# Output stores on ScalarE's queue, v loads on GpSimd's queue, SyncE's queue left to SBUF transposes, 16 matmul groups ahead

## The chip, the cores and the metric

One core of one Trainium2 chip. The metric is the time of one execution on the device in microseconds; a statement about a kernel is the median of several executions, or a ratio of executions taken in the same rounds on the same chip. An execution more than 1.5% above the fastest of the same kernel counts as slow here.

Some words used below: a hole is a stretch in which TensorE stands idle; a transfer lands when its completion semaphore is raised, and its landing time runs from issue to landing; half clock is a stretch in which the profile shows TensorE's granted clock at 0.5 (in before the median from start to start of the MLP's first-layer matmuls is 427 ns there and 216 ns at full clock); `vp` is GpSimd's multiplication of a pair's v by its weights; `osb` are the buffers of finished output tiles that the stores read.

## The reference

Attention with random features (8 batches x 8 heads, 576 tokens, head size 64, 128 features), whose output goes straight into a two-layer MLP over all 4608 tokens.

```python
def phi(x):
    proj = np.einsum('bhsd,md->bhsm', x, omega)
    h = proj - np.sum(x * x, axis=-1, keepdims=True) / 2.0
    h = h - np.max(h, axis=-1, keepdims=True)
    return np.exp(h) / np.sqrt(m)
q_p, k_p = phi(q_s), phi(k_s)
kv  = np.einsum('bhsm,bhsd->bhmd', k_p, v)
z   = np.sum(k_p, axis=2)
num = np.einsum('bhsm,bhmd->bhsd', q_p, kv)
den = np.einsum('bhsm,bhm->bhs', q_p, z)[..., None] + 1e-06
x   = (num / den)                       # -> (4608, 512)
h   = x @ w_in                          # 512 -> 2048
out = (h / (1 + np.exp(-1.702 * h))) @ w_out
```

## The kernel before

The 64 heads are worked as 32 pairs. Each pair needs its q and k transposed before the projection `K`/`Q` on TensorE. Pairs 0 to 7 are transposed by TensorE itself; from pair 8 (`TDMA`) on, SyncE transposes q,k from SBUF to SBUF by DMA (`TD`), and the attention output x as well (`XD`). k, q and the weights are loaded, and cast to bf16, by GpSimd's DMA queue; v (fp32) comes mostly on SyncE's queue, which also carries the output stores.

```python
XDMA, TDMA = 8, 8
...
LOADS += [(x, i) for i in range(8, NPAIR) for x in "kq"]     # GpSimd's order of loads
...
    for n, x in enumerate(LOADS):
        deps["ld", *x] = [("ld", *LOADS[n - 1])] if n else []
        if x[0] in "kq" and x[1] >= 8:                       # 8 buffers for q,k
            deps["ld", *x] += [("TD" if x[1] - 8 >= TDMA else "TQ", x[1] - 8)]
...
        def load_k(i):
            qk_t[i] = stq.tile([128, 2 * S], BF16, name="qk", tag="qk")
            nc.gpsimd.dma_start(qk_t[i][:, S : 2 * S], kv[i])
...
        def TD(i):
            t = qkp.tile([128, NS, 128], BF16, name="qkT", tag="qkT")
            st[i]["qkT"] = t
            nc.sync.dma_start_transpose(t[:], qk_t[i][:])
...
            elif kind == "vp":
                vp(a[0], eng)
                if a[0] + 8 < NPAIR:
                    load_v(a[0] + 8)                         # on SyncE
```

A static scheduler, run while the program is built, models each engine and fixes the order of all instructions. It interleaves the attention of coming pairs with the matmul groups of the MLP (9 blocks of 512 tokens), to keep TensorE full. `TD` of a pair may be placed only so many MLP groups ahead of the pair's due point (6 before, 16 after).

The softmax here doesn't subtract the row's maximum and nothing guards it: scores larger than these inputs give would overflow.

## Time and profile before

| | kernel before |
|---|---|
| time | 337.92 us, median of 3 (337.44 to 338.74) |
| profiled execution | span 340.0 us, TensorE busy 312.9 us, mean clock 0.984 |
| idle of TensorE up to its last matmul | 21.9 us, of which 5.27 before pair 8 |
| half clock of TensorE | 6.8 us from 62.6 us on |

The median transpose lands in 3.4 us. The tile's own view between 43 and 62 us (the first two transposes) gives another size, and the timeline of GpSimd (start us, us, what, and in brackets the idle time before it and who ended it) shows the loads that stood beside them:

```profile
L405 SPq DMA_TRANSPOSE qkT<-qk x2: 2341/3421/4501, 55.4 to 57.9; - x2
DMA to landing us min/median/max: 7.5/8.2/9.0
```
```profile
54.73 0.53 POOL L380 DMA_DIRECT2D qk<-in_k_dram  x1 [0.43 <-issue]
55.76 0.53 POOL L383 DMA_DIRECT2D qk<-in_q_dram  x1 [0.50 <-DMA qk<-in_q_dram]
64.93 0.53 POOL L380 DMA_DIRECT2D qk<-in_k_dram  x1 [8.64 <-DMA qkT<-qk]
```

Near the loads a transpose takes 7.5 to 9 us, not 3.4. And GpSimd issues no load from 56.3 to 64.9 us: the next k needs the buffer that this very transpose reads. While SyncE's transpose is under way, GpSimd's queue gets nothing new; the last load in it landed at 63.85 us.

### The profile page before, as it was taken

What the parts mean: (1) busy time and instruction counts of PE and PEld (TensorE: products, weight loads), DVE (VectorE), ACT (ScalarE), POOL (GpSimd) and SP (SyncE); (2) the same over time, 40 slices, a digit from 0 to 9 for tenths busy, and PEclk for the clock granted to TensorE, in tenths of its full rate; (3) what the DMA queues carried; (4) which work ended last, traced back from release to release, by engine and by line L of the source; (5) the groups of instructions that cost most, each with busy time, mean ns of one, the idle gap of its engine ahead of it and who ended that gap; (6) DMA issues with size and microseconds to landing.
All of it is one profiled execution on the core that took longest, in us unless ns stands there. A gap on an engine that the chain in (4) does not pass through costs nothing.

```text
span 340.0 us, 6567 instructions
## 1 busy us (share of the span) xinstructions
PE 312.9 (92%) x2516; PEld 152.9 (45%) x2562; DVE 181.6 (53%) x336; ACT 192.2 (57%) x353; POOL 79.7 (23%) x137
## 2 busy tenths in 40 slices
PE   5778999499978999999999999999999999999993
PEld 2444554144433445444444444444444444444441
DVE  2786985168854664555555555555564333334400
ACT  3766884286854676666666666666664444444411
POOL 7636423325431242222222111111110000000000
PEclk9899999699999999999999999999999999999999
DMA  7999999999999799686799444444422121112122
GB/s 199 286 222 269 198 221 247 179 149 218 157 186 157 139 175 197 133 160 142 143 135 179 93 87 85 89 85 87 85 53 50 39 55 31 33 31 61 31 64 62
DMA packets 68078, 44.27 MB, mean 130 GB/s; under 512 B 47504, under 2 KB 59536, under 8 KB 68048
## 3 DMA queue, kind: packets, MB, share of 16 engines
q1 hardware_dynamic: 54336, 28.46, 41.0%
q0 software_dynamic: 13712, 15.41, 27.4%
q8 instruction: 20, 0.33, 0.4%
q14 instruction: 10, 0.08, 0.1%
HBM read 36.73 MB, written 9.44 MB: 136 GB/s over the span
## 4 chain that ended last, share of the span: by engine, by line
PE 81%; DMA 9%; DVE 4%; ACT 2%; issue 2%; POOL 1%; ACTq 0%; DVEq 0%; POOLq 0%
PE mo L577 36%; PE mo L597 34%; DMA qkT<-qk 5%; PE pqk L448 3%; PE nd L539 3%; DMA qk<-in_q_dram 2%; PE pqk L477 2%; PE nd L521 2%; DMA xt<-xb 2%; DVE hm L492 1%; DVE xb L556 1%; PE tr L566 1%; ACT xt L428 1%; DVE m L496 0%; PE nd L453 0%
## 5 line engine op out<-in xcount | busy, mean ns | idle before, releaser
L591 DVE SCALAR_TENSOR_TENSOR gT<-th,mo 128x512 bf16<-128x512 bf16 x144 | 97.4, 679 | 99.5 <-ACT th L587 99.3
L577 PE MATMUL mo<-xt,win 128*128 128x512 bf16 x556 | 146.4, 383 | 3.7 <-DMA xt<-xb 1.4
L597 PE MATMUL mo<-wout,gT 128*128 128x512 bf16 x553 | 141.7, 381 | 2.2 <-DVE gT L591 0.9
L587 ACT ACTIVATE th<-mo 128x512 bf16<-128x512 f32 x144 | 86.1, 600 | 75.0 <-PE mo L577 73.0
L597 PEld LDWEIGHTS <-gT 128*128 128x128 bf16 x576 | 55.2, 98 | 67.4 <-issue 2.3
L577 PEld LDWEIGHTS <-win 128*128 128x128 bf16 x576 | 52.6, 98 | 63.7 <-issue 7.2
L486 ACT ACTIVATE qe<-pqk 128x1024 bf16<-128x1024 f32 x28 | 28.7, 1024 | 9.4 <-PE pqk L477 9.4
L466 ACT ACTIVATE ke<-pqk 128x1024 bf16<-128x1024 f32 x32 | 33.1, 1034 | 0.0
L510 POOL TENSOR_TENSOR vp<-v,em 128x576 bf16<-128x576 f32 x27 | 31.1, 1152 | 0.0
L380 POOL DMA_DIRECT2D qk<-in_k_dram x31 | 17.5, 565 | 55.6 <-DMA qkT<-qk 47.9
L607 ACT ACTIVATE osb<-mo 128x512 f32<-128x512 f32 x36 | 21.5, 598 | 15.6 <-PE mo L597 12.4
L509 POOL CAST vp<-em 128x9 bf16<-128x9 f32 x27 | 6.4, 236 | 101.1 <-DVE em L501 94.1
L556 DVE TENSOR_TENSOR xb<-nd,r 128x640 bf16<-128x640 f32 x30 | 24.7, 823 | 0.9
L496 DVE TENSOR_REDUCE m<-hm 128x9 f32<-128x576 bf16 x32 | 24.0, 749 | 0.3
L492 DVE TENSOR_TENSOR hm<-ke 128x576 bf16<-128x576 bf16 x32 | 17.8, 555 | 9.9 <-ACT ke L466 9.8
L457 ACT ACTIVATE ke<-nd 128x128 bf16<-128x128 f32 x32 | 8.9, 278 | 24.8 <-PE nd L454 24.1
L448 PE MATMUL pqk<-omT,qkT 64*128 64x128 bf16 x256 | 13.2, 224 | 7.6 <-DMA qkT<-qk 7.3
L383 POOL DMA_DIRECT2D qk<-in_q_dram x31 | 16.9, 545 | 9.5 <-DMA wout<-in_moe_w_out_dram 5.4
L539 PEld LDWEIGHTS <-qe 128*128 128x128 bf16 x320 | 13.8, 97 | 6.7 <-issue 0.7
L548 DVE RECIPROCAL r<-nd 128x10 f32<-128x10 f32 x30 | 6.4, 214 | 18.8 <-ACT qe L458 13.0
L521 PEld LDWEIGHTS <-ke 64*128 64x128 bf16 x576 | 12.5, 95 | 8.2 <-issue 2.5
L539 PE MATMUL nd<-kvs,qe 128*128 128x65 bf16 x300 | 14.3, 194 | 0.4
(54 smaller groups left out, 149.8 us busy)
## 6 DMA issues: line engine op xcount, KB each, us to landing
out_dram<-osb SPq DMA_DIRECT2D x72, 128.0 KB, 2.4
v<-in_v_dram SPq DMA_DIRECT2D x25, 288.0 KB, 5.5
qk<-in_k_dram POOLq DMA_DIRECT2D x31, 144.0 KB, 6.0
qk<-in_q_dram POOLq DMA_DIRECT2D x31, 144.0 KB, 6.3
win<-in_moe_w_in_dram POOLq DMA_DIRECT2D x4, 512.0 KB, 12.0
wout<-in_moe_w_out_dram POOLq DMA_DIRECT2D x4, 512.0 KB, 11.6
v<-in_v_dram POOLq DMA_DIRECT2D x7, 288.0 KB, 8.7
qkT<-qk SPq DMA_TRANSPOSE x24, 3.4
```

Source lines behind the costliest of these rows:

```text
L448: nc.tensor.matmul(pk[:, e, j * 128 : (j + 1) * 128], lhsT=t[64 * e : 64 * e + 64, k0 + j, :], rhs=omT[64 * e : 64 * e + 64, :],)
L466: nc.scalar.activation(out=st[i]["ke"][:, 1:9, :].rearrange("p (j e) f -> p e j f", e=2), in_=pk[:].rearrange("p e (j f) -> p e j f", f=12 ...
L486: nc.scalar.activation(out=dst, in_=src, func=AF.Exp, scale=SCALE)
L496: nc.vector.reduce_max(out=m[:], in_=st[i]["hm"][:], axis=AX.X)
L510: e.tensor_tensor(out=t[:, :, 0:64], in0=v_t[i][:], in1=em[:].unsqueeze(2).to_broadcast([128, NS, 64]), op=ALU.mult,)
L539: nc.tensor.matmul(nd[:, e, g * 65 : (g + 1) * 65], lhsT=qe[i % NQE][:, e, g * 128 : (g + 1) * 128], rhs=t[:, e, :],)
L556: nc.vector.tensor_tensor(out=xb[:].rearrange("p g e d -> p e g d"), in0=v4[:, :, :, 0:64], in1=r[:].unsqueeze(3).to_broadcast([128, 2, NG ...
L577: nc.tensor.matmul(dst, lhsT=win[:, c, f * 128 : (f + 1) * 128], rhs=xt[c][:, n * 512 : (n + 1) * 512], start=(c == 0), stop=(c == NC_ - 1),)
L587: nc.scalar.activation(out=t[:], in_=src, func=AF.Tanh, scale=0.851)
L591: nc.vector.scalar_tensor_tensor(out=gts[n][:, f, :], in0=t[:], scalar=1.0, in1=src, op0=ALU.add, op1=ALU.mult)
L597: nc.tensor.matmul(dst, lhsT=gts[n][:, f, r * 128 : (r + 1) * 128], rhs=wout[:, f, :], start=(f == 0), stop=(f == NFC - 1),)
L607: nc.scalar.activation(out=o[:], in_=src, func=AF.Copy, scale=0.5)
```

## The change

Intent: give SyncE's queue to the transposes alone, so that they go as soon as their data is there; start them earlier; and let loads and stores find their own queues. Core of the diff (hunk headers and some context left out):

```diff
+NOSB = 4
+NQK = 6
-LAT = {..., "S": 4.0}
+LAT = {..., "S": 3.0}
-    "TD": {"S": 0.6},
-    "XD": {"S": 0.6},
+    "TD": {"S": 2.1},
+    "XD": {"S": 1.2},
+    "st": {"A": 0.2},
-LOADS += [(x, i) for i in range(8, NPAIR) for x in "kq"]
+LOADS += [(x, i) for i in range(8, NPAIR) for x in "kqv"]
-            deps["TD", i] = ... + p("Q", i - 4) + p("K", i - 4) + l("k") + l("q")
+            deps["TD", i] = ... + p("Q", i - NQK) + p("K", i - NQK) + l("k") + l("q")
+                deps["st", n, r] = [("store", n, r)]
+        if x[0] == "v" and x[1] >= 8:
+            deps["ld", *x] += [("vp", x[1] - 8)]
-        if kind in ("TK", "TD") and begin[o[1]] - (6 if kind == "TD" else 0) > st["m"]:
+        if kind in ("TK", "TD") and begin[o[1]] - (16 if kind == "TD" else 0) > st["m"]:
-    qkp = ctx.enter_context(tc.tile_pool(name="qkp", bufs=4))
+    qkp = ctx.enter_context(tc.tile_pool(name="qkp", bufs=NQK))
-    osbp = ctx.enter_context(tc.tile_pool(name="osb", bufs=3))
+    osbp = ctx.enter_context(tc.tile_pool(name="osb", bufs=NOSB))
+        def send(n, r):
+            o = osb.pop((n, r))
             u = 2 * (4 * n + r)
             for h in range(2):
                 b, rank = divmod(u + h, NS)
-                nc.sync.dma_start(ov[b, SLOT[rank]], o[64 * h : 64 * h + 64, :])
+                nc.scalar.dma_start(ov[b, SLOT[rank]], o[64 * h : 64 * h + 64, :])
                 vp(a[0], eng)
-                if a[0] + 8 < NPAIR:
-                    load_v(a[0] + 8)
```

More of the change, by code (lines that the diff above doesn't have):

```diff
@@ L28 @@
 NQE = 4
+NOSB = 4
+NQK = 6
 NPAIR = B * 4
 SCALE = 1.0 / math.sqrt(math.sqrt(D))
-LAT = {"P": 0.26, "A": 0.20, "D": 0.16, "G": 0.20, "S": 4.0}
+LAT = {"P": 0.26, "A": 0.20, "D": 0.16, "G": 0.20, "S": 3.0}
 SELF = {"P": 0.0, "A": 0.11, "D": 0.13, "G": 0.10, "S": 0.0}
@@ L90, in schedule @@
         if i >= TDMA:
-            deps["TD", i] = (p("TD", i - 1) if i > TDMA else []) + p("Q", i - 4) + p("K", i - 4) + l("k") + l("q")
+            deps["TD", i] = (p("TD", i - 1) if i > TDMA else []) + p("Q", i - NQK) + p("K", i - NQK) + l("k") + l("q")
             t = p("TD")
@@ L149, in schedule @@
             if g == 3:
-                deps["store", n, r] = [o]
+                deps["store", n, r] = [o] + ([("st", *divmod(4 * n + r - NOSB, 4))] if 4 * n + r >= NOSB else [])
+                deps["st", n, r] = [("store", n, r)]
     for n, x in enumerate(LOADS):
         deps["ld", *x] = [("ld", *LOADS[n - 1])] if n else []
+        if x[0] == "v" and x[1] >= 8:
+            deps["ld", *x] += [("vp", x[1] - 8)]
         if x[0] in "kq" and x[1] >= 8:
@@ L603, in m2 @@
                 )
+        osb = {}
         def store(n, r, src):
             o = osbp.tile([128, DM], F32, name="osb", tag="osb")
+            osb[n, r] = o
             nc.scalar.activation(out=o[:], in_=src, func=AF.Copy, scale=0.5)
+        def send(n, r):
+            o = osb.pop((n, r))
             u = 2 * (4 * n + r)
@@ L680, in emit @@
                 {"KV": KV, "kvs": kvs, "ND": ND, "rd": rd, "xm": xm}[kind](a[0], t)
+            elif kind == "st":
+                send(*a)
             elif kind in ("TD", "XD"):
```

## The prediction

> **What bounds the kernel now.** I read the page first, its slices and then the chain. TensorE (PE) is busy 312.9 of 340.0 us, so only its idle or slow stretches are to be had; and the slices say where they lie.
>
> ```profile
> PE   5778999499978999999999999999999999999993
> PEclk9899999699999999999999999999999999999999
> DMA  7999999999999799686799444444422121112122
> ```
>
> A slice is 8.5 us. PE is below 9 in the first four, in the eighth (4 tenths, at a granted clock of 0.6), in the twelfth and in the thirteenth. From 110 us on it is full to the end. The DMA row is full over just the stretch where PE has holes. I then cut the span at the holes (columns: PE, PEld, DVE, ACT, POOL busy with counts, granted clock, DMA share and GB/s):
>
> ```profile
> 59.20:64.50 5.30, 0.06 (x2) 0.06 (x4) 0.00 (x0) 0.65 (x1) 0.00 (x0) 0.82 1.28 178
> 64.50:69.50 5.00, 5.00 (x21) 2.04 (x22) 1.36 (x3) 1.96 (x4) 2.65 (x5) 0.51 1.03 190
> 69.50:110.00 40.50, 35.49 (x373) 17.23 (x378) 27.48 (x50) 26.51 (x52) 14.05 (x23) 1.00 1.11 172
> 110.00:255.00 145.00, 143.40 (x1219) 71.12 (x1241) 84.43 (x157) 93.34 (x173) 32.42 (x52) 1.00 0.65 122
> ```
>
> One hole of 5.3 us, then 5.0 us of work at half clock, then 5.0 us of idleness spread over 40 us, then 1.6 us in 145. [...] Who ended the holes is in the waits of PE (total us, times, longest) and in the chain of waits (start, us, what):
>
> ```profile
> PE pqk L448 <- DMA qkT<-qk: 7.3, 2, 5.3
> PE mo L577 <- DMA xt<-xb: 1.4, 1, 1.4
> ```
> ```profile
> 55.42 8.98 DMA qkT<-qk
> 88.53 8.32 DMA qkT<-qk
> 100.29 5.66 DMA xt<-xb
> ```
>
> All three are SBUF transposes issued by SyncE: two of q,k (5.27 us before the work of pair 8, 2.04 us at 94.9), one of x (1.40 us at 104.6). The timeline of SyncE and GpSimd shows why the first came so late:
>
> ```profile
> 2.13 48.09 SPq L387 DMA_DIRECT2D v<-in_v_dram  x8
> 52.54 2.09 SPq L611 DMA_DIRECT2D out_dram<-osb  x2
> 54.74 0.51 SPq L387 DMA_DIRECT2D v<-in_v_dram  x1
> 55.42 9.26 SPq L405 DMA_TRANSPOSE qkT<-qk  x3
> ```
> ```profile
> 37.33 0.61 POOL L380 DMA_DIRECT2D qk<-in_k_dram  x1
> 37.93 0.55 POOL L383 DMA_DIRECT2D qk<-in_q_dram  x1
> ```
>
> The last two rows are k and q of pair 8; by the trace's landing events they arrived at 49.58 and 50.31. Their transpose could have gone then. It went at 55.42 (the first of the three merged in that row), because SyncE's queue is in order and first held a v load that waited for another pair's `vp`, two stores that waited for `osb`, and another v load. Then it took 8.98 us to land, against a median of 3.4 for this group, beside eight loads in flight.
>
> [...] So I expect nothing from bandwidth here, only from the order in SyncE's queue. The trace agrees so far as the lateness above was queue order. [...] the 5.27 us hole is followed by 0.51, the holes of 2.04 and 1.40 us by nothing. [...]
>
> **The change part by part.**
>
> *SyncE keeps only the 48 transposes.* It loses 72 store issues and 24 of its 25 v loads. The first transpose of pair 8 is then bound by its data. Six v loads (pairs 8 to 13, 295 KB each, 1.77 MB) no longer run before 50 us: loads of this size land 0.7 us apart at the quick stretches (pairs 6 and 7), so k and q of pair 8 arrive about 6 x 0.7 = 4 us earlier, near 46 us (estimate). With even 9 us to land, the transpose is there at 55, before PE asked for it at 59.2. So the 5.27 us hole goes (-5.3), and with it the half clock: 5.0 us of work at 0.51 becomes 2.5 (-2.5).
>
> *16 groups ahead, six buffers.* A matmul group of the MLP is 0.86 us, so 10 groups more are 8.6 us of earlier start, if k,q have landed and a buffer is free; six instead of four buffers permit it for pairs 8 to 13. I note that the static scheduler gates only the transpose by this number, not the projection K after it: K is placed as soon as the modelled transpose is over (2.1 + 3.0 us, before 0.6 + 4.0). So the attention of a pair moves ahead as a whole, and the room between transpose and use grows by only 0.5 us. What protects PE is that x of a block is ready some 8 us earlier: the 1.40 us wait for xt should go (-1.4). The 2.04 us wait should go because SyncE spent 86.7 to 94.6 on v, stores and transposes in turn, that transpose's own issue stretching to 2.90 us (-2.0).
>
> *v in the Pool queue, in the order k, q, v.* 24 issues of 0.55 us (row of GpSimd's v loads, 542 to 579 ns) are 13 us on an engine that is busy 79.7 of 340. It puts a v load, which waits for `vp` of eight pairs before, ahead of the next k; with about 8.4 us per pair and eight pairs in hand that wait is hidden. At the start it helps: today v of pairs 8, 9 and 10 is fetched at 2.6 to 13.2 us, ahead of q of pair 2, for which PE waits 1.15 us at 11.24. I count half of it (-0.6).
>
> *Stores on ScalarE.* Two issues of 0.47 to 0.59 us per tile, 1.12 us together, 36 times: 40 us more on ScalarE, busy 192.2, so 232 of 330, no bound by itself. What counts is how late it makes the next tanh. In the steady state a tanh follows the store's copy after 0.27 us idle; it would start about 0.9 us later. The PSUM bank that it frees is wanted again 1.66 us after its release there, and 0.86 us after it in the last 80 us. I worked these slacks out from the starts of L577 and the ends of L591 by bank. So the delay just fits[...]. The schedule reckons 0.2 us for what takes 1.1, so it won't plan around it: +1.0 in sum. *Four osb buffers* only let a store be sent later; 0.
>
> Late transposes that remain in the crowded 60 to 110 us: +1.5, from three landings of 7.5 to 10.5 us today among the first eight, of which only some hit PE.
>
> Sum: -5.3 -2.5 -2.0 -1.4 -0.6 +1.0 +1.5 = -9.3; 337.9 - 9.3 = 328.6 us.
>
> **Rivals.** *A: the waits come back elsewhere.* The DMA share is at 1.0 to 1.3 up to 110 us, and the change moves no byte out of the program: with attention 8 us earlier, transposes and loads crowd still more, and K is still placed 5.1 us behind its transpose. Against it: the six v loads leave the tightest stretch, and MLP work of block 1 is there to fill. It would leave 334 to 336. *B: ScalarE becomes the bound.* [...] tanh is 2.5 us late, over the 1.66 us of slack, and PE loses up to 0.8 us in each of some 17 periods between 110 and 255 us (8.42 us apart: store copies start at 197.69 and 206.11): up to +14, that is 338 to 342. For it: the phase is that close today. Against: the schedule shifts the phase, and one tight row seldom repeats so exactly. *C: no cost at all* (-11.8): 326.1, and 324 to 325 if the small waits for gT (0.64 and 0.25 us at 81 and 100 us) go too.
>
> **Range and chances.** The sure part is the hole and the clock, 7.8 us, by itself 2.3%: 330.1. The other gains (2.0, 1.4, 0.6) are 4.0, against costs that I put at 2.5 and that A or B could make 8. I put the 8-in-10 range at 324 to 336. Faster by over 2% means under 331.2; the middle lies 2.6 us below, so 0.67; same 0.29; slower 0.04, for B at its full.
>
> **What would show it.** Right: [...] PEclk at 9 throughout after the start; the first q,k transpose issued before 50 us; SyncE with 48 issues after its first few; waits of PE for qkT under 2 us in sum; ScalarE's stretch from 110 to 255 us with PE still 143 of 145. Wrong: a half-clock stretch again near 60 to 70 us (A), or PE gaps of 0.3 to 0.8 us before L577 and L597 released by gT once per period, with store issues over 1 us on ScalarE (B).

That spreading the issues would change nothing in bandwidth was my estimate. So was rival B's tanh "2.5 us late": two issues of 1.2 to 1.3 us in a row, as SyncE's transposes took at 197.5 and 198.9 us; that a store on ScalarE would be held behind them was not shown. Of the clock, before's trace shows half clock from 62.62 to 69.44 us, begun within the 5.27 us hole, and none behind the holes of 2.04 and 1.40 us.

## More of the kernel before

The prediction shows the slices, the hole and the chain. Some views that it doesn't show matter for what follows. The first is the page's list of DMA issues (tile, queue, kind, count, KB each, median us from issue to landing):

```profile
v<-in_v_dram SPq DMA_DIRECT2D x25, 288.0 KB, 5.5
v<-in_v_dram POOLq DMA_DIRECT2D x7, 288.0 KB, 8.7
qkT<-qk SPq DMA_TRANSPOSE x24, 3.4
```

## The result, and the profile after

| | before, same rounds | after |
|---|---|---|
| time | 338.27 us, median of 4 (337.44 to 338.74) | 354.2 us, median of 4 (347.33, 348.11, 360.29, 362.35) |
| ratio of fast runs | | 1.0282, 95% interval 1.0239 to 1.0326: slower |
| profiled execution (fast) | span 340.0 us | span 345.6 us |

A ratio here and below is the mean time of one kernel's fast runs over the mean of the other's in the same rounds, so it is not quite the ratio of the medians that are quoted; here the median of after mixes two fast and two slow runs. Everything below about the kernel after is from its profiled run, a fast one. The profiled execution of before took 341.91 us, 3.7 us more than the mean of its runs in these rounds, so the two profiles below differ by less than the 9.5 us of the ratio.

The slices (tenths busy, the granted clock in tenths) and the DMA issues after:

```profile
PE   6888996468998999999999999999999999999994
PEclk9899999659999999999999999999999999999999
DMA  8999999999999999889774454624221112111222
qkT<-qk SPq DMA_TRANSPOSE x24, 4.7
```

There is now a weak stretch of three slices of TensorE, the seventh to the ninth (6, 4 and 6 tenths), with a reduced clock in the eighth and ninth (0.6 and 0.5); the DMA engines are at 9 tenths or more from the second slice to the sixteenth. The median transpose went from 3.4 to 4.7 us. The same stretches as in the prediction's table, but cut at 80 us (PE, PEld, DVE, ACT, POOL busy with counts, granted clock, DMA share, GB/s), first of before, then of after:

```profile
59.20:80.00 20.80, 15.35 (x115) 6.94 (x118) 10.08 (x19) 12.12 (x25) 7.35 (x14) 0.84 1.19 171
80.00:110.00 30.00, 25.20 (x279) 12.39 (x282) 18.76 (x34) 17.00 (x33) 9.34 (x15) 1.00 1.07 177
```
```profile
59.20:80.00 20.80, 12.10 (x76) 4.66 (x76) 4.61 (x9) 5.97 (x14) 5.01 (x9) 0.67 1.24 159
80.00:110.00 30.00, 27.28 (x290) 13.22 (x290) 20.50 (x40) 21.96 (x43) 19.35 (x34) 1.00 1.23 225
110.00:255.00 145.00, 143.57 (x1249) 69.00 (x1248) 84.79 (x156) 90.82 (x170) 36.05 (x59) 1.00 0.66 123
```

From 59 to 80 us after does 76 matmuls where before did 115; from 80 to 110 us it wins some back; from 110 to 255 us they are the same (143.57 and 143.40 us busy). So the loss is made between 57 and 72 us. The waits of after (total us, times, longest us) and the view of the tile `qkT` for 43 to 62 us name it:

```profile
PE pqk L454 <- DMA qkT<-qk: 5.9, 2, 5.8
PE mo L583 <- ACT xt L434: 4.7, 2, 4.5
```
```profile
L411 SPq DMA_TRANSPOSE qkT<-qk x4: 1940/6751/12917, 44.5 to 60.4; - x4
DMA to landing us min/median/max: 17.6/20.3/23.9
```

The transpose of pair 8 was issued at 44.5 us instead of 55.4, as intended: by the trace's landing events its k and q arrived at 43.63 and 44.38 us (49.58 and 50.31 before). But it landed after 18.94 us, at 63.40, where before it landed at 64.40. Eleven microseconds of earlier issue bought one. The next three took 23.9, 21.7 and 17.6 us. TensorE stood from 57.68 to 63.45 us, and then, after some work, from 67.26 to 71.72 us, now for ScalarE. ScalarE's timeline shows why:

```profile
55.40 0.60 ACT L616 ACTIVATE osb<-mo 128x512 f32<-128x512 f32 x1 [0.54 <-PE mo L603]
63.48 7.49 ACTq L623 DMA_DIRECT2D out_dram<-osb  x2
71.02 0.65 ACT L434 ACTIVATE xt<-tr 128x576 bf16<-128x576 bf16 x1 [15.02 <-DMA out_dram<-osb]
```

Between 56.0 and 71.0 us ScalarE did nothing but issue two stores. By the semaphore records of after, all DMAs of SyncE and ScalarE name one of the same eight completion semaphores (108, 109, 112, 113, 115 to 118), taken in turn in program order; the first store got the semaphore last used by the transpose of pair 8 (115; landed 63.40, the store went at 63.48), the second that of pair 9 (116; landed 70.47, the store went at 70.49). So a slow transpose held ScalarE too, although the store depended on it in nothing else. Between the two holes and behind them TensorE ran at half clock for 13.65 us (before: 6.83 us).

Compared at the last matmul, after ends 6.0 us later (340.85 against 334.82 us). Of this: after is 1.0 us ahead when pair 8 starts (63.45 against 64.44) and saves 4.3 us of before's waits between 81 and 106 us; it loses 4.46 us to the second hole and 3.8 us to smaller waits of its own, and 1.75 us to half clock (of its 13.65 us at half clock it works 8.5, of before's 6.83 us before works 5.0, and at twice the spacing of the matmuls, 427 against 216 ns, half of the difference is lost). That makes 4.7 of the 6.0 us; 1.3 us I could not assign.

What was in the DMA queues is seen in GpSimd's timeline after (`...` marks lines left out). It issues loads, three to a pair, before and behind the first transpose of 44.46 us, eight of them from then to 50.9 us; then none until 58.0 us, with most of those eight still on their way (the first landed at 57.45 us):

```profile
44.19 0.54 POOL L393 DMA_DIRECT2D v<-in_v_dram  x1 [0.45 <-issue]
44.73 0.54 POOL L386 DMA_DIRECT2D qk<-in_k_dram  x1
...
50.35 0.53 POOL L389 DMA_DIRECT2D qk<-in_q_dram  x1 [0.45 <-DMA v<-in_v_dram]
58.00 0.54 POOL L393 DMA_DIRECT2D v<-in_v_dram  x1 [7.11 <-DMA qk<-in_k_dram]
```

### The profile page after: what moved, and what is told of

It is laid out like the page before. It is cut to its first block, busy times and chain, and to the rows that moved or that the text cites. A ratio compares the mean times of both kernels' runs of the same rounds, so it can differ in the third digit from the quotient of the medians.

```text
span 345.6 us, 6563 instructions
## 1 busy us (share of the span) xinstructions
PE 319.4 (92%) x2562; PEld 152.0 (44%) x2562; DVE 180.1 (52%) x336; ACT 191.1 (55%) x353; POOL 92.7 (27%) x161
## 3 DMA queue, kind: packets, MB, share of 16 engines
q10 hardware_dynamic: 5760, 9.44, 11.1%
## 4 chain that ended last, share of the span: by engine, by line
PE 69%; ACT 2%; ACTq 2%; DMA 2%; DVE 1%; issue 1%
PE mo L603 32%; PE mo L583 29%; PE nd L545 2%; PE nd L527 2%; ACTq L623 2%; PE pqk L454 2%; DMA qkT<-qk 2%; PE pqk L483 2%; ACT qe L492 1%; ACT osb L616 1%; ACT ke L472 0%; PE nd L459 0%; DVE xb L562 0%; DVE m L502 0%; DVE gT L597 0%
## 5 line engine op out<-in xcount | busy, mean ns | idle before, releaser
L583 PE MATMUL mo<-xt,win 128*128 128x512 bf16 x576 | 149.1, 383 | 6.2 <-ACT xt L434 4.7
L603 PE MATMUL mo<-wout,gT 128*128 128x512 bf16 x576 | 147.0, 383 | 0.0
L583 PEld LDWEIGHTS <-win 128*128 128x128 bf16 x576 | 53.9, 99 | 70.3 <-issue 12.0
L603 PEld LDWEIGHTS <-gT 128*128 128x128 bf16 x576 | 53.5, 98 | 63.1 <-issue 2.7
L516 POOL TENSOR_TENSOR vp<-v,em 128x576 bf16<-128x576 f32 x27 | 31.0, 1150 | 0.0
L498 DVE TENSOR_TENSOR hm<-ke 128x576 bf16<-128x576 bf16 x32 | 15.5, 484 | 24.2 <-ACT ke L472 24.1
L393 POOL DMA_DIRECT2D v<-in_v_dram x31 | 17.8, 576 | 15.7 <-DMA qk<-in_k_dram 10.4
L454 PE MATMUL pqk<-omT,qkT 64*128 64x128 bf16 x256 | 13.3, 226 | 6.3 <-DMA qkT<-qk 5.9
L434 ACT ACTIVATE xt<-tr 128x576 bf16<-128x576 bf16 x8 | 5.3, 660 | 21.7 <-DMA out_dram<-osb 15.0
L527 PEld LDWEIGHTS <-ke 64*128 64x128 bf16 x576 | 12.4, 96 | 10.1 <-issue 2.8
L554 DVE RECIPROCAL r<-nd 128x10 f32<-128x10 f32 x30 | 6.4, 215 | 18.3 <-PE nd L545 11.7
```

The lines of the kernel that those rows point to most:

```text
L454: nc.tensor.matmul(pk[:, e, j * 128 : (j + 1) * 128], lhsT=t[64 * e : 64 * e + 64, k0 + j, :], rhs=omT[64 * e : 64 * e + 64, :],)
L516: e.tensor_tensor(out=t[:, :, 0:64], in0=v_t[i][:], in1=em[:].unsqueeze(2).to_broadcast([128, NS, 64]), op=ALU.mult,)
L583: nc.tensor.matmul(dst, lhsT=win[:, c, f * 128 : (f + 1) * 128], rhs=xt[c][:, n * 512 : (n + 1) * 512], start=(c == 0), stop=(c == NC_ - 1),)
L603: nc.tensor.matmul(dst, lhsT=gts[n][:, f, r * 128 : (r + 1) * 128], rhs=wout[:, f, :], start=(f == 0), stop=(f == NFC - 1),)
```

## The experiments

Two theories stood at first. In the one (H in the expectations), the long hold of ScalarE by its stores is the loss. In the other (M, later P), the landing time of the transposes is: it grows when loads are under way. P adds that transposes and loads then move about as many packets per us (measured in `micro`, below), and a transpose has many small ones (1184 in the trace's packet records, 1152 of them of 256 B, against 144 for a k or q load and 80 for a v load on GpSimd's queue). All whole-kernel runs gave correct outputs. Holes and landing times in the text are from each run's gaps on TensorE and its landing events.

### Each part alone

`b_st`: before, with the stores alone on ScalarE (with their own scheduler entry and four `osb`).

```diff
-                nc.sync.dma_start(ov[b, SLOT[rank]], o[64 * h : 64 * h + 64, :])
+                nc.scalar.dma_start(ov[b, SLOT[rank]], o[64 * h : 64 * h + 64, :])
```

> The kernel before with the stores alone moved to ScalarE (and four osb buffers). Theory H (ScalarE is held: the stores' completion semaphores are a ring of eight shared with SyncE's transposes, so a store waits until a transpose issued earlier has landed, and everything behind it on ScalarE waits too): ScalarE shows waits of several us before stores released by a transpose, and the kernel is slower than before, 340 to 346 us. Theory M (the loss comes from transposes landing late beside the loads, and the stores on ScalarE are harmless): same as before or a little faster, 335 to 339, since SyncE is freer.

The ring that theory H names is the eight semaphores of after's records above; there ScalarE's two stores stood 7.5 and 6.5 us for it.

Measured: 341.28 us, ratio 1.0104 [1.0061, 1.0146]. First transpose issued at 54.4 us, landed after 10.7; the hole stays (59.45 to 65.10 us). No store waited for a transpose's semaphore here (one waited 1.75 us for that of a v load). So the time lies in the range of theory H, but the wait that H expected is absent.

`b_v`: before, with the v loads alone on GpSimd's queue.

```diff
-LOADS += [(x, i) for i in range(8, NPAIR) for x in "kq"]
+LOADS += [(x, i) for i in range(8, NPAIR) for x in "kqv"]
+        if x[0] == "v" and x[1] >= 8:
+            deps["ld", *x] += [("vp", x[1] - 8)]
-                if a[0] + 8 < NPAIR:
-                    load_v(a[0] + 8)
```

> The kernel before with the v loads alone moved to the Pool queue. Theory M (transposes issued while the Pool queue is full of loads crawl): the transposes of pairs 8 to 10 land in 12 us or more, against 9.0 before, and the kernel is 340 us or slower. Theory H: no store on ScalarE, so no hold, 333 to 338.

Measured: 343.46 us, 1.0144 [1.0085, 1.0203]. The time is as theory M expected, the landings are not: pairs 8 to 10 landed after 7.6, 5.8 and 3.4 us. The first hole is smaller (3.07 us), but a transpose issued at 74.5 us took 18.3 us and made another of 10.7 us. Its PE wait:

```profile
PE pqk L450 <- DMA qkT<-qk: 14.7, 4, 10.7
```

`b_ahead`: before, with 16 groups ahead, six buffers and the scheduler's new costs alone.

```diff
-        if kind in ("TK", "TD") and begin[o[1]] - (6 if kind == "TD" else 0) > st["m"]:
+        if kind in ("TK", "TD") and begin[o[1]] - (16 if kind == "TD" else 0) > st["m"]:
-    qkp = ctx.enter_context(tc.tile_pool(name="qkp", bufs=4))
+    qkp = ctx.enter_context(tc.tile_pool(name="qkp", bufs=NQK))     # NQK = 6; the costs are left out here
```

> The kernel before with 16 groups ahead, six q,k buffers and the changed costs of the scheduler, stores and v loads left where they were. Theory M: SyncE's queue still delays the first transpose to about 50 us or later, so little is changed, 335 to 341. Theory H: no hold either, the same range; if it is 345 or more, the new order of the instructions alone is the cause and both theories fall.

Measured: 344.55 us, 1.0196 [1.015, 1.0242]. First transpose at 56.1 us only (SyncE's queue still holds it), several smaller holes of 0.9 to 3.5 us, most of them waits for transposes. This is slower than the 335 to 341 us of both theories, just short of the 345 us at which both were to fall.

`a_stsp`: after, with the stores back on SyncE.

```diff
-                nc.scalar.dma_start(ov[b, SLOT[rank]], o[64 * h : 64 * h + 64, :])
+                nc.sync.dma_start(ov[b, SLOT[rank]], o[64 * h : 64 * h + 64, :])
```

> The changed kernel with the stores issued by SyncE again, at the same place of the order. Theory H: ScalarE no longer waits 7 and 6.5 us at 56 to 63 and 64 to 70 us, and the time falls to 336 to 341. Theory M alone: the first transpose still lands near 63 us and PE stands still as long as before, 345 to 349.

Measured: 350.1 us median, 1.0235 [1.0146, 1.0323] for the fast runs; its profile fell in a slow run, so only its pattern is used: the first three transposes took 13.2 to 17.4 us, and TensorE waited for them four times. ScalarE could not be held here.

What follows: every part loses by itself, the three don't add up (1.010, 1.014, 1.020 against 1.028 together), and the ScalarE hold is not the main cause: without it, the loss is nearly the same and comes as waits for the transposes themselves. The first theory falls as the whole story.

### Transposes beside loads, by themselves

`micro`: no kernel, only transposes and loads of this kernel's shapes in stretches with barriers between, some alone and some together. Its output is wrong, which doesn't matter for the time.

```diff
+        for i in range(12):          # and the same without T, without cast, with plain v loads (flat)
+            cast(i)                  # a k,q-sized load on GpSimd's queue
+            if i % 3 == 0:
+                T(i // 3)            # a TD on SyncE's queue
+        barrier(lb + dst)
...
+        for i in range(4):
+            sp(i)                    # a double v load on SyncE's queue
+            T(i)
```

> The transfers by themselves, result wrong on purpose (zeros stored): nine stretches with a barrier between: 4 q,k transposes alone; 12 cast loads of 295 KB from the Pool queue alone; both together; 12 loads of v without cast from the Pool queue alone; with 4 transposes; 4 double v loads from ScalarE's queue alone; with 4 transposes from SyncE; 4 such loads and 4 transposes in turn on SyncE's one queue; stores on ScalarE alone and with transposes. Theory M (transposes and loads on different queues disturb each other beyond sharing): the transposes alone take about 8 us, the 12 loads alone about 10 us, and together over 25 us. Rival S (they only share the engines' time): together 18 us or less, and the long landings in the kernel have another cause.

Measured: four transposes alone took 7.6 us in all, each 3.3 to 3.4. 12 cast loads alone took 13.3, both together 19.3: about the sum (20.9), nothing is lost. But the transposes landed after 5.2, 12.1, 14.6 and 9.0 us. Beside 12 plain v loads (12.7 us alone, 23.5 together, 3.2 more than the sum) they landed after 5.5, 17.1, 19.5 and 11.8. Four double v loads and four transposes in turn on SyncE's one queue: 13.9 us in all, landings 4.5 to 5.8. The stretches with stores overlapped one another and are not used. Both times lie between the ranges of the two theories (18 us or less, over 25 us), so neither is decided. What is seen is that a landing grew from 3.4 us alone to as much as 14.6 us beside the cast loads and 19.5 us beside the v loads.

`micro2`: how does the time divide? One transpose at the head of a queue of loads; four, each waiting for the one before; four that don't wait.

```diff
+        stretch(None, 1, {0: [0]})                                       # comments added here
+        stretch(cast, 12, {0: [0]})
+        stretch(cast, 12, {0: [0], 3: [1], 6: [2], 9: [3]}, same=True)   # one target tile: each waits
+        stretch(cast, 12, {0: [0], 3: [1], 6: [2], 9: [3]})              # and all with flat for cast
```

> Transfers by themselves again, result wrong on purpose, nine stretches with a full barrier after each: one transpose alone; one beside 12 cast loads; one beside 12 uncast loads, both from the Pool queue; four transposes each waiting for the one before to land, beside 12 cast loads, then beside 12 uncast; four not waiting, beside 12 cast, then 12 uncast; one beside 6 uncast loads from ScalarE's queue; one beside 4 stores. Theory P [...]: a transpose of some 1150 packets lands after 3.4 us alone, 8 to 10 us beside cast loads (155 packets a us in the first measurement) and 12 to 14 us beside uncast loads of 4.6 KB packets (97 a us). Rival C (a collapse only when two transposes are in flight at once): one transpose or waiting ones land in 4 to 6 us, those in flight together in over 12.

The 8 to 10 and 12 to 14 us are estimates, from some 1150 packets at the 155 and 97 per us of `micro`.

Measured: one alone 3.29 us. One at the head of 12 cast loads 4.10 us, of 12 v loads 5.36 us: less than the 8 to 10 and 12 to 14 us expected, but it was issued 0.4 and 0.65 us ahead of the first load. Of four that wait for each other, the second, which starts in the midst of 12 cast loads, took 9.33 us (issued at 64.55, landed at 73.88); amid 12 v loads 12.97 us; once the loads were through, again 3.2. Four that don't wait took 5.7, 12.1, 13.4 and 6.7 us beside cast loads, 6.3, 15.8, 17.8 and 12.1 beside v loads. So a single transpose amid loads is late too, which rival C did not expect (4 to 6 us); those behind another are later still. The tile's view from 58 to 75 us:

```profile
L109 SPq DMA_TRANSPOSE dst<-src x3: 1281/1297/1338, 58.8 to 73.9; - x3
DMA to landing us min/median/max: 3.2/5.7/9.3
```

The packet records show the rates: with both under way, cast loads and transposes each moved 149 to 161 packets per us (beside v loads 96 to 100 each, at 142 to 144 us; elsewhere in that stretch they are uneven); alone, the transposes of `micro` moved about 800 per us. At equal rates a transpose with 1184 packets lasts as long as 1184 load packets, that is as 8 k or q loads of 144, or 15 v loads of 80, if so many are waiting (an estimate from these counts). For cast loads equal rates are shown, and the rival, that loads and transposes cost each other extra, falls (19.3 us together, 20.9 in sum alone); beside v loads the 3.2 us above the sum speak for some extra cost.

In the changed kernel these rates are not the whole account. From 47 to 63 us GpSimd's loads moved 57 and transposes 116 packets per us, 136 GB/s in sum, where the joint stretch of `micro` has 196 GB/s (54 to 58 us, cast loads). At 155 or 98 packets per us, 1184 packets would take about 8 or 12 us (an estimate), not 18.94, and the loads that GpSimd issued from 44.7 to 50.4 us took 12.7 to 16.7 us to land. What slowed both there stays unexplained.

### In the kernel: where, how many, how big

`b_t12`: before, with TensorE transposing pairs 8 to 11 too, so that SyncE's first transposes come after the thickest loads.

```diff
-XDMA, TDMA = 8, 8
+XDMA, TDMA = 12, 12
```

> The kernel before with the transposes of pairs 8 to 11 (q,k and x) done by TensorE as those of pairs 0 to 7 are, so that none is in flight while the Pool queue is full of loads. Theory M: the hole of 5.3 us and the half clock go, 4 pairs of TensorE transposes cost about 3 us; 328 to 334. Rival S: the loads themselves are late then and the holes stay, 337 or more.

The 3 us for four pairs are an estimate; in before's trace five such transposes took 0.28 us of TensorE (at 41.40 us) and four 0.22 us (at 45.64 us).

Measured: 332.29 us, 0.9792 [0.9744, 0.9841]. No hole over 1.3 us, no half clock after the start:

```profile
59.20:80.00 20.80, 20.27 (x231) 11.58 (x234) 15.68 (x33) 16.09 (x33) 11.12 (x19) 1.00 0.98 180
80.00:110.00 30.00, 29.74 (x300) 15.27 (x303) 18.47 (x36) 21.34 (x41) 8.55 (x14) 1.00 0.80 154
```

`a_t12`: the same edit in after.

```diff
-XDMA, TDMA = 8, 8
+XDMA, TDMA = 12, 12
```

> The changed kernel with the same edit. Theory M: the two holes and the half clock go and the time falls by 12 us or more against the changed kernel, to 325 to 335; ScalarE's hold goes too, as it hung on late transposes. Theory H' (issuing stores from ScalarE costs by itself): it stays 3 us or more above the other kernel of this set. Rival S: 344 or more.

Measured: 337.51 us, 0.9951 [0.9882, 1.002]. The same edit repairs most of after too, though less than the 325 to 335 us expected: it stays 5.2 us above `b_t12`, as theory H' had it. Its transposes of 67.9 and 70.2 us still took 11.1 and 14.5 us. How much of the 5.2 us is theirs and how much a cost of the new queues as such is not separated here.

`a_6`: after, with 6 groups ahead in place of 16.

```diff
-        ... begin[o[1]] - (16 if kind == "TD" else 0) > st["m"]:
+        ... begin[o[1]] - (6 if kind == "TD" else 0) > st["m"]:
```

> The changed kernel with transposes 6 groups ahead again instead of 16. Theory M: the first transpose still meets the loads at 44 us (it is bound by its data there), the next three come later; 341 to 347. If the early issue is the whole cause: 338 or less.

Measured: 362.91 us, 1.0559 [1.0492, 1.0626], a miss: I had expected it better than after. The first transpose was issued at 44.5 us all the same (its loads decide, not the 16), and the first five landings took 19 to 31 us (a slow run). So taking the 16 groups back does not mend the changed kernel; without them it is worse.

`a_vsp`: after, with v back on SyncE's queue.

```diff
-LOADS += [(x, i) for i in range(8, NPAIR) for x in "kqv"]
+LOADS += [(x, i) for i in range(8, NPAIR) for x in "kq"]
-        if x[0] == "v" and x[1] >= 8:
-            deps["ld", *x] += [("vp", x[1] - 8)]
                 vp(a[0], eng)
+                if a[0] + 8 < NPAIR:
+                    load_v(a[0] + 8)
```

> The changed kernel with the v loads back in SyncE's queue, as in the kernel before. Theory P: the Pool queue holds cast loads alone, so the first transposes land in 8 to 14 us in place of 19 to 24; 338 to 345 us. If the v loads in the Pool queue do not matter: 347 or more.

Measured: 341.99 us, 1.0101 [1.0058, 1.0143]. Of the parts taken out of after, v's place on GpSimd's queue gives the most back; added alone to before, though, the 16 groups ahead cost more (1.0196 against 1.0144). The edit also moves the first transpose: it is late again (54.6 us), lands after 10.1, and the hole is 5.05 us.

`a_vcast`: after, with v cast to bf16 while it is loaded. In after's records the cast k and q loads have packets of 1152 B, the uncast v loads of 4608 B; that a cast v load would look like the former was my estimate. If the size of the v packets were the matter, the transposes would land sooner.

```diff
-            t = stv.tile([128, NS, D], F32, name="v", tag="v")
+            t = stv.tile([128, NS, D], BF16 if eng is nc.gpsimd else F32, name="v", tag=...)
```

> The changed kernel with v cast to bf16 on its way in, so that its packets in the Pool queue are as small as those of q and k; nothing else changed. Theory P: the first transposes land in 10 to 15 us in place of 19 to 24 and the time falls to 337 to 345. If packet size is not it: 347 or more, landings as before.

Measured: 356.41 us, 1.0467 [1.0401, 1.0532], a miss for theory P, which expected 337 to 345 (its profile is a slow run). Only the first landing fell (13.8 us); the next were 21.1, 21.7 and 16.7. So the cast is no help.

`b_t10`: before, with 10 in place of 8.

```diff
-XDMA, TDMA = 8, 8
+XDMA, TDMA = 10, 10
```

> The kernel before with the DMA transposes beginning at pair 10 in place of 8 (12 gave 332.3). Theory P: the transposes of pairs 10 and 11 still meet a full Pool queue, so a hole of 1 to 4 us is left; 332 to 336.

Measured: 338.31 us, 0.9986 [0.9923, 1.0049]. The hole moved and grew (62.73 to 69.54 us); GpSimd, held at a load that waited for a transpose, was late with a `vp`. This fits the view that what matters is how full the load queue is when the first transpose goes: here it took 12.1 us.

### Holding the loads back

All this was by way of the loads' amount and place. The direct test keeps everything in after and only lets fewer loads stand beside a transpose.

`a_gate2`: after, with k of pair i, from pair 10 on, waiting until the transpose of pair i-2 has landed. The wait is a one-element copy on GpSimd that reads the transposed tile; the scheduler is told of it, so that its order of instructions shifts a little as well.

```diff
         if x[0] in "kq" and x[1] >= 8:
             deps["ld", *x] += [("TD" if x[1] - 8 >= TDMA else "TQ", x[1] - 8)]
+        if x[0] == "k" and x[1] - 2 >= TDMA:
+            deps["ld", *x] += [("TD", x[1] - 2)]
+        gate = const.tile([1, 1], BF16, name="gate")
         def load_k(i):
+            if i - 2 >= TDMA:
+                nc.gpsimd.tensor_copy(out=gate[:], in_=st[i - 2]["qkT"][0:1, 0, 0:1])
```

> The kernel after, with one edit: the load of k for pair i, from pair 10 on, waits on GpSimd until the transpose of pair i-2 has landed, so that at most two pairs of loads stand beside a transpose (no transpose is issued later in the program, v stays on the Pool queue, stores on ScalarE). Theory P [...]: the transposes of pairs 8 and 9, which in the kernel after took 18.9 and 23.9 us, land within 12 us, pair 8 before 57 us; the hole of 5.77 us and the ScalarE hold behind it go, and the time is 335 to 344 us. Rival L (the load volume is the limit, whoever goes first): the held loads arrive later by as much as the transposes gain, the holes come back as waits for transposes of pairs 10 to 13 issued late, and the time stays at 345 us or above.

What stands of theory P are the equal rates of `micro` (149 to 161 packets per us each).

Measured: 333.67 us, 0.9852 [0.9799, 0.9904]: later loads, and the shift in order that comes with them, make the changed kernel some 4% faster (0.9852 over 1.0282). GpSimd's timeline, the tile's view and the stretch from 59 to 80 us:

```profile
38.46 0.60 POOL L399 DMA_DIRECT2D v<-in_v_dram  x1
47.84 0.49 POOL L390 COPY gate<-qkT 1x1 bf16<-1x1 bf16 x1 [8.79 <-DMA qkT<-qk]
48.28 0.53 POOL L392 DMA_DIRECT2D qk<-in_k_dram  x1
```
```profile
L417 SPq DMA_TRANSPOSE qkT<-qk x4: 1277/1439/1834, 43.8 to 56.1; - x4
DMA to landing us min/median/max: 3.3/4.2/5.7
```
```profile
59.20:80.00 20.80, 19.09 (x193) 9.52 (x196) 15.19 (x29) 15.24 (x32) 8.08 (x16) 1.00 0.76 125
```

The same four transposes, the first three issued within 1.7 us of their times in after, the fourth 4.3 us earlier, land in 3.3 to 5.7 us instead of 17.6 to 23.9. Both holes and the half clock between them are gone, and from 54 to 82 us no pair of store issues takes ScalarE more than 1.9 us. The rival, that the volume of loads is the limit whoever goes first, falls.

`a_gate4`: the same with i-4 and pair 12, so that more loads stand beside a transpose.

```diff
+        if x[0] == "k" and x[1] - 4 >= TDMA:
+            deps["ld", *x] += [("TD", x[1] - 4)]
+            if i - 4 >= TDMA:
+                nc.gpsimd.tensor_copy(out=gate[:], in_=st[i - 4]["qkT"][0:1, 0, 0:1])
```

> The same with i-4 in place of i-2 and pair 12 in place of pair 10: four pairs of loads may stand beside a transpose. Theory P: pairs 8 and 9 still land late (12 to 18 us, because the loads of pairs 8 to 11 are in the queue with them), later ones within 10 us; time between the two, 340 to 347 us. Rival L: the same as the kernel after, 346 to 349 us.

Measured: 342.28 us median; its runs spread from 334.78 to 346.37, so that only one counts as fast and no ratio is given. Landings of the first four (profile in a slow run) are between those of after and of `a_gate2`, as expected:

```profile
DMA to landing us min/median/max: 9.4/10.5/12.7
```

A later transpose took 15.2 us and left a hole of 7.79 us at 94.2 us. ScalarE is idle there from 95.4 to 103.1 us, but not held by a store: its two store issues took 1.12 us, and what it did next waited for TensorE. The longest wait of a store for a transpose's semaphore was 2.9 us, at 59.29. So the large loss of this slow run is a late landing without ScalarE; of the faster runs there is no trace.

`b_gate2`: the gate of `a_gate2`, the same lines, in before.

```diff
+        if x[0] == "k" and x[1] - 2 >= TDMA:
+            deps["ld", *x] += [("TD", x[1] - 2)]
+            if i - 2 >= TDMA:
+                nc.gpsimd.tensor_copy(out=gate[:], in_=st[i - 2]["qkT"][0:1, 0, 0:1])
```

> The kernel before with the same gate as in the run that gated the kernel after (k of pair i, from pair 10 on, waits on GpSimd for the landing of the transpose of pair i-2). If the three parts of the change are worth something once the transposes land early (theory: the prediction was right but for the landing time), this stays slower than the gated kernel after: its transposes are still issued late (about 55 us) and behind v loads and stores, 336 to 341 us. Rival: the gate alone is the gain and the change's parts are worth nothing: 331 to 335 us here too.

Measured: 333.65 us, 0.9831 [0.9773, 0.9888]. I expected 336 to 341; the rival was right. The transposes are still issued late, behind v and the stores, and that costs nothing:

```profile
L411 SPq DMA_TRANSPOSE qkT<-qk x2: 1242/1529/1816, 55.8 to 57.8; - x2
DMA to landing us min/median/max: 3.2/3.5/3.8
```

Issued 0.4 us later than in before (55.78 against 55.42), the first lands at 59.6 instead of 64.4 us, and the hole before pair 8 is gone (one of 2.05 us is left at 80.9 us). With the gate, before and after run equally fast (333.65 and 333.67 us, each against before in its own rounds): in this pair the three parts of the change, taken together, are worth nothing once the transposes land quickly.

### Looking for a better version

`b_t16`: before, with 16 in place of 8.

```diff
-XDMA, TDMA = 8, 8
+XDMA, TDMA = 16, 16
```

> The kernel before with the first transpose by SyncE at pair 16 (TensorE does pairs 8 to 15 too). With 12 the time was 332.3 us and no hole was over 1.3 us, so nothing is left to win from holes there: four more pairs cost TensorE about 9 transposes and two evictions a pair. Expected: the same as with 12 or slower, 332 to 336 us. If it is under 331 us, transposes from pairs 12 to 15 still cost something in the version with 12.

Measured: 343.78 us, 1.0141 [1.0078, 1.0203], a miss. Its transposes land in 3.2 to 5.8 us and no wait is over 2 us, yet TensorE is busy only 136.12 of the 145 us from 110 to 255 us (`b_t12`: 143.46). Where those 7 us go I did not follow up.

`b_t12g` and `a_t12g`: the gate (from pair 14 on) in `b_t12` and in `a_t12`.

```diff
-XDMA, TDMA = 8, 8
+XDMA, TDMA = 12, 12
+        if x[0] == "k" and x[1] - 2 >= TDMA:
+            deps["ld", *x] += [("TD", x[1] - 2)]
+            if i - 2 >= TDMA:
+                nc.gpsimd.tensor_copy(out=gate[:], in_=st[i - 2]["qkT"][0:1, 0, 0:1])
```

> The version with the first SyncE transpose at pair 12 and the gate from pair 14 on. It had transposes of up to 12 us left at 52 to 75 us but no hole over 1.3 us, so the gate can win little: 330 to 333 us, ratio to before 0.975 to 0.985. Rival: a gate costs GpSimd waits that delay v products: 334 us or more.

> The kernel after with the first SyncE transpose at pair 12 and the gate from pair 14 on. Without the gate it was 337.5 us, its transposes took up to 14.5 us and it had one wait of 1.4 us; with it, if the landing times were what cost, 330 to 335 us. If it stays at 337 us, the 5 us that separate it from the kernel before with pair 12 come from something other than landing times.

Measured: `b_t12g` 332.02 us, 0.9798 [0.9737, 0.9859], the same as `b_t12`: where loads no longer meet transposes, holding them back wins nothing. (The 12 us that the expectation ascribes to `b_t12` are not in its trace; its slowest transpose took 6.8.) `a_t12g` 336.83 us, 0.9934 [0.9886, 0.9983], short of the 330 to 335 that I expected. One transpose, issued at 135.4 us, took 7.5 us and made TensorE wait 1.92 us, with 3.4 us of half clock behind it; that is 3.6 of the 5.7 us by which its last matmul is later than that of `b_t12g`. The rest is open, and so is whether the changed queues cost something of their own: the gate alone put before and after level, with 12 in place of 8 after stays 5 us behind. The best versions are `b_t12` and `b_t12g`, 2% better than before and 5% better than after, without any part of the change.

## Why the prediction was wrong

**What bounds before: half right.** The three waits and the half clock were the loss to look at; those of 2.04 and 1.40 us did go in after, as said. But the prediction explained the lateness of the first transpose by SyncE's order, and called the 8.98 us to land an addition. `b_gate2` turns this round: same late issue, quick landing, no hole. So the late issue alone does not make the hole; the late landing does. What the prediction read of the clock from before alone, half clock with the hole of 5.27 us and none with 2.04 and 1.40, does not carry over either: half clock also came behind holes of 2.05 us in `b_gate2` (from 83.1 us) and 1.92 us in `a_t12g` (from 144.2 us), where before's hole of 2.04 us had none.

**The step that failed**: "With even 9 us to land, the transpose is there at 55, before PE asked for it at 59.2. So the 5.27 us hole goes (-5.3), and with it the half clock". Its first half was right: data at 44.4 us, even earlier than the 46 predicted, and issue at 44.46. The 9 us was carried over from before as if it belonged to the transpose. It belongs to the loads beside it. Before landed in 9 us because GpSimd, waiting for that transpose, sent no load after 56.3 us. After issued the transpose among loads that came three to a pair, with v in between, and it took 18.94 us. The packet records give the difference: between the issue and the landing of this transpose 746 load packets of GpSimd's queue went by in before, 1195 in after, 194 in `a_gate2` (3.95 us) and none in `b_gate2` (3.84 us). The -5.3 became 0 (a hole of 5.77 us, begun 1.5 us earlier), the -2.5 became a loss, since half clock doubled.

**The term "late transposes that remain, +1.5"** was mis-sized: the second hole (4.46 us) and after's smaller waits (3.8 us) stand in its place. The second hole came in a way that the prediction didn't have: a store on ScalarE held by the completion semaphore of a late transpose. In `a_gate2`, where transposes land early, the stores are still on ScalarE and the hold is gone; so it needs the late landings and is no cause of its own. How much of the 2.8% goes through it stays open, since `a_stsp`, without it, loses about as much in other waits.

**Stores on ScalarE (+1.0)**: nearer 0 in the steady stretch, where TensorE was busy 143.57 of 145 us against 143.40. Rival B (ScalarE becomes the bound, up to +14 us) didn't occur. **The head (-0.6)**: right in kind; pair 8 was reached 1.5 us earlier and the wait for q of pair 2 fell from 1.15 to 0.64 us. **Rival A** named the right place (transposes and loads crowd still more), but as a wait of the same size moved elsewhere, 334 to 336 us. The argument against it, that six v loads leave the tightest stretch, failed: GpSimd issued five of them between 36.98 and 48.83 us.

**Range and chances.** The "sure part" of 7.8 us was the least sure: it rested on one landing time that the prediction itself had seen to be 2.6 times the median and had put down to the loads in flight. Had it asked what the change does to those loads, it would have found v added to that queue and the issue moved into its fullest time. With the gate the changed kernel runs in 333.67 us, inside the range of 324 to 336; but that is the gate's gain, since `b_gate2` has it without the change.

**Open**: 1.3 us of the 6.0 us between the two profiles; the stretch from 47 to 63 us, in which DMA moved less than in `micro` (136 against 196 GB/s); why half of after's runs are 13 us slower than the others (the slow profiles of the variants show later landings, but no run tells why).

## What to carry to other kernels

A landing time read from a profile belongs to the traffic beside it (the same transpose took 8.98, 18.94, 3.95 and 3.84 us in before, after, `a_gate2` and `b_gate2`): before you issue a many-packet transfer earlier, ask which queues will be full at that moment and what kept them empty until now. If a small transfer is on the critical path and a bulk load isn't, make the loads wait for it (a wait of one element was enough here, for 1.7% in before and 4% in after), in place of moving the small one to a queue of its own. And before crediting a change with a hole, try the cheapest edit that removes the same hole without it.
